# The output product in seven block products with w_out stationary, and sums of h read out of one accumulating bank

## The chip, the cores and the metric

The kernel runs on one core of a Trainium2 chip. The metric is device time in microseconds (us) of one execution. Every execution is put in a state, fast or slow, by its time and the clock that the throttle granted TensorE. PE is TensorE, PEld its weight loads, DVE VectorE, ACT ScalarE, POOL GpSimd. PSUM is the memory that TensorE writes its products into; this kernel uses it as eight banks of 128 x 512 fp32.

## The reference, cut to what matters

A causal convolution of 7 taps (weights by head, softmax over taps), then a two-layer block with Silu, all in fp32:

```python
B, S, D = 8, 4096, 192;  d_ff = 2048          # 32768 tokens
out[b, s] = sum_k softmax(weight)[h, k] * x_pad[b, s + k]      # 7 taps, h = head of the column
h = x @ w_in                                   # (32768,192) @ (192,2048)
g = h * (1.0 / (1.0 + np.exp(-h)))
return (g @ w_out).astype(np.float32)          # (32768,2048) @ (2048,192)
```

## The kernel before

It works in 32 blocks of 1024 tokens. "Up" is the first layer, "down" the second. Up already uses a scheme in which a 2x2 block product takes seven products instead of eight; each product has 64 rows, and two of them run side by side on the halves of the array (in the trace of this kernel both records of a pair start at 1034.82 us, the next pair at 1035.25, 0.43 later). A "slot" is such a pair. VectorE adds the products up from several PSUM banks. Down is plain, with g stationary and w_out moving. In the lines of the profile `ps` is a PSUM bank, `dup` and `win` hold the convolved input and sums of it, `wr` and `ws` come from w_in, `wo` and `wx` from w_out.

```python
gpool = ctx.enter_context(tc.tile_pool(name="gp", bufs=NCH))
upool = ctx.enter_context(tc.tile_pool(name="up", bufs=6))
psum = ctx.enter_context(tc.tile_pool(name="ps", bufs=8, space=PSUM))
# ...
def up_pair(b, j):                       # one of 4 groups of a block: 11 slots
    # P1, P2, E11 in bank "b"; P7, P4, E21 in "c"; P6 in "a"; P5, E22, P3, E12 in "d"
    def after(e, name):
        if name == "P1":
            us[e, 2] = upool.tile([P, TB], F32, tag="u", name="u")
            nc.scalar.copy(us[e, 2], bk[e, "b"])
        elif name == "U2":
            add(us[e, 2], us[e, 2], bk[e, "a"])
        elif name == "U3":
            us[e, 3] = upool.tile([P, TB], F32, tag="u", name="u")
            add(us[e, 3], us[e, 2], bk[e, "c"])
        # ... E22, E21, E12: add(g, us, bank), then Silu in place
# ...
def down(b):
    for i, c in enumerate(order):        # 16 chunks of d_ff
        g = gs.pop((b, c)).rearrange("p n t -> p (n t)")
        for s in range(SUBS):            # 8 times 128 tokens
            nc.tensor.matmul(accs[s // 2][:, s % 2, :], g[:, ts(s, P)], wo[c // 4][:, c % 4, :], ...)
# ...
for b in range(NB):
    # up of b; then turn_in(b+1), load(b+2), conv(b+1), win(b+1); then
    accs = down(b)
    store(b, accs)
```

A tile pool with `bufs=n` hands out n buffers in turn; whoever wants the next one waits until its last reader is done. And the program's text is not the order in which an engine runs: the compiler's scheduler orders each engine's queue itself, within the dependences.

Of the kernel before, what the change touches and what calls it, by code (L numbers as in the profile page):

```python
# [1 line left out]

# [14 lines left out]
def kernel(  # L17
# [22 lines left out]

    nc = tc.nc
# [13 lines left out]
    SUBS = TT // P  # L55
# [8 lines left out]
    out_v = out.rearrange("(n s p) d -> n p s d", s=SUBS, p=P)  # L64

    const = ctx.enter_context(tc.tile_pool(name="const", bufs=1))
    wpool = ctx.enter_context(tc.tile_pool(name="wp", bufs=1))
    xpool = ctx.enter_context(tc.tile_pool(name="xp", bufs=1))
    gpool = ctx.enter_context(tc.tile_pool(name="gp", bufs=NCH))
    upool = ctx.enter_context(tc.tile_pool(name="up", bufs=6))  # L70
    psum = ctx.enter_context(tc.tile_pool(name="ps", bufs=8, space=PSUM))

# [3 lines left out]
    nats, xts, cvs, gs = {}, {}, {}, {}  # L76
# [23 lines left out]
    out32 = moe_w_out.bitcast(I32).rearrange("(q e p) d -> q p e d", e=4, p=P)  # L100
    wr = [const.tile([P, 2, NK, P], F32, name=f"wr{j}") for j in range(NJ)]
    ws = [const.tile([P, 2, NK, P], F32, name=f"ws{j}") for j in range(NJ)]
    wo = [const.tile([P, 4, D], F32, name=f"wo{q}") for q in range(NCH // 4)]
    raws = {}

    def raw_tile(key):
        raws[key] = wpool.tile([P, 2 * WC], I32, tag="raw", name="raw", bufs=2)
        return raws[key]
# [10 lines left out]
    def load_out(q, queue):  # L119
        raw = raw_tile(("o", q))  # L120
        queue.dma_start(out=raw.rearrange("p (e d) -> p e d", e=4), in_=out32[q])

    def rounded(dst, key):
        words = raws.pop(key).rearrange("p (n t) -> p n t", t=2)
        lo, hi = words[:, :, 0], words[:, :, 1]
        ex, st, mh = (
            wpool.tile([P, WC], I32, tag=f"w_{n}", name=f"w_{n}") for n in ("ex", "st", "mh")
        )
# [37 lines left out]
    def round_out(q):  # L166
        rounded(wo[q].rearrange("p e d -> p (e d)"), ("o", q))

    def combine(j):


        def comb(out, u, v, op):
            nc.gpsimd.tensor_tensor(out, u, v, op=op)  # L173

        s, r = ws[j], wr[j]
        comb(s[:, 1, 0, :], s[:, 1, 0, :], s[:, 1, 1, :], ALU.add)
        comb(s[:, 0, 0, :], s[:, 1, 0, :], s[:, 0, 0, :], ALU.subtract)
        comb(s[:, 0, 1, :], s[:, 0, 1, :], s[:, 0, 0, :], ALU.subtract)
        comb(s[:, 0, 2, :], s[:, 0, 2, :], s[:, 1, 2, :], ALU.subtract)
        comb(r[:, 1, 0, :], r[:, 0, 0, :], r[:, 1, 0, :], ALU.subtract)  # L180

# [43 lines left out]
    def turn_in(b):  # L225
        nat = nats.pop(b)
# [5 lines left out]
        for k in range(NK):  # L232
            nc.vector.transpose(  # L233
                xt[:, k, pad : pad + TB], nat[:, k, :, :].rearrange("p k c -> p (k c)")
            )
        nc.sync.dma_start(out=xt[R:P, :, 0:pad], in_=xt[0:R, :, TB : TB + pad])
# [4 lines left out]
    def conv(b, k):  # L241
        if k == 0:
            cvs[b] = xpool.tile([P, NK, TB], F32, tag="cv", name="cv")
            dups[b] = xpool.tile([P, 2, NK, TB], F32, tag="dup", name="dup")
        src, dst = xts[b][:, k, :], cvs[b][:, k, :]
        for i in range(K):
            tap = taps[:, k, i : i + 1]
            if i == 0:
                nc.vector.tensor_scalar(dst, src[:, 0:TB], scalar1=tap, scalar2=None, op0=ALU.mult)
            else:  # L250
                nc.vector.scalar_tensor_tensor(  # L251
                    out=dst, in0=src[:, i : i + TB], scalar=tap, in1=dst, op0=ALU.mult, op1=ALU.add
                )
        for n in range(2):
            for e in range(2):
                nc.sync.dma_start(
                    out=dups[b][R * e : R * e + R, n, k, :], in_=cvs[b][R * n : R * n + R, k, :]
# [19 lines left out]
    def g_tile(b, c):  # L277
        if (b, c) not in gs:
            gs[b, c] = gpool.tile([P, 2, TB], F32, tag="g", name="g")
        return gs[b, c]  # L280

    def up_plain(b, j):
# [7 lines left out]
        for k, (a, n) in order:  # L290
# [8 lines left out]
            if k == NK - 1:  # L299
                for e in range(2):  # L300
                    g = g_tile(b, NM * a + 2 * j + e)
                    nc.scalar.activation(g[:, n, :], hs[a, n, e], AF.Silu)

    def up_pair(b, j):
        d, t = dups[b], wins[b]
        r, s = wr[j], ws[j]

        prods = {
            "P1": (0, r[:, 0, 0, :], d[:, 0, 0, :], "b", True),
            "P2": (0, r[:, 0, 1, :], d[:, 0, 1, :], "b", False),  # L310
            "E11": (0, r[:, 0, 2, :], d[:, 0, 2, :], "b", False),
            "P7": (0, r[:, 1, 0, :], t[:, 2, :], "c", True),
            "P4": (0, r[:, 1, 1, :], t[:, 3, :], "c", False),
            "E21": (0, r[:, 1, 2, :], d[:, 0, 2, :], "c", False),
            "P6": (1, s[:, 0, 0, :], t[:, 1, :], "a", True),
            "P5": (1, s[:, 1, 0, :], t[:, 0, :], "d", True),
            "E22": (1, s[:, 1, 2, :], d[:, 1, 2, :], "d", False),
            "P3": (1, s[:, 0, 1, :], d[:, 1, 1, :], "d", False),
            "E12": (1, s[:, 0, 2, :], d[:, 1, 2, :], "d", False),
        }  # L320
        bk, us = {}, {}

        def mm(e, name):
            other, w, v, bn, first = prods[name]
            half = e ^ other
            if first:
                bk[e, bn] = bank()
            nc.tensor.matmul(  # L328
                bk[e, bn], rows(w, half), rows(v, half), start=first, stop=True,
                skip_group_check=True,  # L330
            )

# [3 lines left out]
        def after(e, name):  # L336
            top, low = 2 * j + e, NM + 2 * j + e
            if name == "P1":
                us[e, 2] = upool.tile([P, TB], F32, tag="u", name="u")
                nc.scalar.copy(us[e, 2], bk[e, "b"])  # L340
            elif name == "E11":
                nc.scalar.activation(g_tile(b, top)[:, 0, :], bk[e, "b"], AF.Silu)  # L342
            elif name == "U2":
                add(us[e, 2], us[e, 2], bk[e, "a"])
            elif name == "U3":
                us[e, 3] = upool.tile([P, TB], F32, tag="u", name="u")
                add(us[e, 3], us[e, 2], bk[e, "c"])
            else:
                c, n, u, bn = {
                    "E22": (low, 1, 3, "d"), "E21": (low, 0, 2, "c"), "E12": (top, 1, 2, "d")  # L350
                }[name]
                g = g_tile(b, c)[:, n, :]
                add(g, us[e, u], bk[e, bn])
                nc.scalar.activation(g, g, AF.Silu)  # L354



        for slot, then in (
            (((0, "P1"), (0, "P6")), ((0, "P1"),)),
            (((0, "P7"), (0, "P5")), ((0, "U2"), (0, "U3"))),  # L360
            (((1, "P6"), (1, "P1")), ((1, "P1"),)),
            (((1, "P5"), (0, "E22")), ((0, "E22"), (1, "U2"))),
            (((1, "E22"), (1, "P7")), ((1, "U3"), (1, "E22"))),
            (((0, "P2"), (1, "P2")), ()),
            (((0, "E11"), (0, "P3")), ((0, "E11"),)),
            (((0, "P4"), (0, "E12")), ((0, "E12"),)),
            (((0, "E21"), (1, "E11")), ((0, "E21"), (1, "E11"))),
            (((1, "P3"), (1, "P4")), ()),
            (((1, "E12"), (1, "E21")), ((1, "E12"), (1, "E21"))),
        ):  # L370
            for e, name in slot:
                mm(e, name)
            for e, name in then:
                after(e, name)

    def down(b):


        accs = [bank()[:, 0 : 2 * D].rearrange("p (s d) -> p s d", s=2) for _ in range(SUBS // 2)]
        order = [NM * a + m for m in range(NM) for a in range(2)]  # L380
        for i, c in enumerate(order):
            g = gs.pop((b, c)).rearrange("p n t -> p (n t)")
            for s in range(SUBS):
                nc.tensor.matmul(  # L384
                    accs[s // 2][:, s % 2, :],
                    g[:, ts(s, P)],
                    wo[c // 4][:, c % 4, :],
                    start=i == 0 and s % 2 == 0,
                    stop=i == NCH - 1,
                    skip_group_check=True,  # L390
                )
        return accs

    def store(b, accs):
        osb = xpool.tile([P, SUBS, D], F32, tag="osb", name="osb")
        for i, acc in enumerate(accs):
            part = osb[:, 2 * i : 2 * i + 2, :]
            if i % 2:
                nc.scalar.copy(part, acc)  # L399
            else:  # L400
                nc.vector.tensor_copy(part, acc)  # L401
        for i in range(2):
            nc.sync.dma_start(out=out_v[b][:, 4 * i : 4 * i + 4, :], in_=osb[:, 4 * i : 4 * i + 4, :])

    turn_in(0)
    load(1)
    conv(0, 0)
    for b in range(NB):
        for j in range(NJ):
            if b == 0:  # L410
                round_in(j)
                if j == 0:
                    for k in range(1, NK):
                        conv(0, k)
# [4 lines left out]
                up_plain(b, j)  # L419
            else:  # L420
                up_pair(b, j)
        if b == 0:
            for q in range(NCH // 4):
                round_out(q)
                if q + 2 < NCH // 4:
                    load_out(q + 2, nc.gpsimd)
# [42 lines left out]
```

## Time and profile before

| | before |
|---|---|
| time, median of 3 runs | 2644.91 us (2644.26 to 2645.23) |
| span of the profiled run, granted clock | 2640.4 us, 0.995 |
| up of one block / down of one block | 38.30 / 41.80 us |
| VectorE busy in a block's up, down (stretches of 38.4 and 41.8 us) | 24.95, 20.29 us |

Read it as: TensorE is the bound in both stages (busy for 38.40 of 38.40 and 41.80 of 41.80 us), and VectorE is idle for 35% of up and about half of down. The lines that say so are in the prediction.

### The profile page before, as it was taken

How to read it: one execution, taken by the hardware profiler on the slowest of the kernel's cores; microseconds unless marked ns; L12 is line 12 of the kernel's file. 1: busy time of each engine (PE TensorE's matmuls, PEld its weight loads, DVE VectorE, ACT ScalarE, POOL GpSimd, SP SyncE). 2: the span in 40 equal slices, each digit the busy share in tenths (PEclk: the TensorE clock that was granted, in tenths of full speed). 3: DMA queues.
4: the chain of work that ended last, by engine and by line, in shares of the span. 5: the costliest groups of instructions: out<-in, count | busy, mean ns of one | idle time of the engine just before them, and what ended most of it. 6: DMA issues, size and time to landing. Idle time of an engine off the chain costs nothing.

```text
span 2640.4 us, 34007 instructions
## 1 busy us (share of the span) xinstructions
PE 2576.4 (98%) x13840; PEld 2045.2 (77%) x13840; DVE 1466.8 (56%) x2270; ACT 780.4 (30%) x1355; POOL 33.7 (1%) x77
## 2 busy tenths in 40 slices
PE   2899999999999999999999999999999999999999
PEld 1777887778887778887778877788877788877788
DVE  7655556555556455556455565555564555564532
ACT  1332223332223332233322233322233322233222
POOL 3000000000000000000000000000000000000000
PEclk9899999999999999999999999999999999999999
DMA  7311211112211212211112211112112122111010
GB/s 150 67 42 31 49 45 33 44 28 46 49 34 39 49 25 49 49 34 40 40 34 48 47 32 43 30 43 49 34 40 49 24 49 49 34 40 34 15 37 13
DMA packets 282220, 111.04 MB, mean 42 GB/s; under 512 B 222160, under 2 KB 255696, under 8 KB 282064
## 3 DMA queue, kind: packets, MB, share of 16 engines
q1 hardware_dynamic: 278912, 100.98, 17.6%
q0 software_dynamic: 1536, 5.51, 0.8%
q10 hardware_dynamic: 1616, 2.39, 0.4%
q8 instruction: 109, 1.79, 0.3%
q14 instruction: 47, 0.39, 0.0%
HBM read 31.49 MB, written 25.17 MB: 21 GB/s over the span
## 4 chain that ended last, share of the span: by engine, by line
PE 97%; DMA 1%; DVE 1%; POOL 0%; ACT 0%; issue 0%; ACTq 0%; SPq 0%; DVEq 0%; POOLq 0%
PE ps L384 51%; PE ps L328 45%; PE ps L292 1%; DVE cv L251 1%; DMA raw<-in_moe_w_in_dram 0%; DMA nat<-in_x_dram 0%; DMA ws<-wr 0%; DMA raw<-in_moe_w_out_dram 0%; POOL ws L173 0%; DMA xt<-xt 0%; DVE w_ex L151 0%; POOL raw L115 0%; DVE w_mh L148 0%; DVE xt L233 0%; DVE w_ex L132 0%
## 5 line engine op out<-in xcount | busy, mean ns | idle before, releaser
L384 PEld LDWEIGHTS ps<-wo,g 128*128 128x128 f32 x8192 | 1330.3, 190 | 24.3 <-issue 24.3
L384 PE MATMUL ps<-wo,g 128*128 128x192 f32 x8192 | 1339.8, 326 | 0.0
L328 PE MATMUL ps<-dup,wr 64*128 64x512 f32 x1984 | 736.9, 591 | 0.0
L328 PE MATMUL ps<-dup,ws 64*128 64x512 f32 x1488 | 679.8, 591 | 0.0
L334 DVE TENSOR_TENSOR g<-u,ps 128x512 f32<-128x512 f32 x744 | 491.4, 684 | 231.6 <-PE ps L328 227.2
L354 ACT ACTIVATE g<-g 128x512 f32<-128x512 f32 x744 | 461.6, 630 | 415.1 <-DVE g L334 414.7
L328 PE MATMUL ps<-win,wr 64*128 64x512 f32 x992 | 505.0, 589 | 0.0
L328 PEld LDWEIGHTS ps<-dup,wr 64*128 64x128 f32 x1984 | 308.9, 187 | 201.0 <-issue 138.0
L334 DVE TENSOR_TENSOR u<-u,ps 128x512 f32<-128x512 f32 x496 | 331.9, 685 | 185.3 <-ACT u L340 170.5
L328 PE MATMUL ps<-win,ws 64*128 64x512 f32 x992 | 427.1, 592 | 0.0
L399 ACT COPY osb<-ps 128x384 f32<-128x384 f32 x64 | 30.6, 478 | 1271.7 <-PE ps L384 1271.7
L251 DVE SCALAR_TENSOR_TENSOR cv<-xt,taps,cv 128x512 f32<-128x512 f32 x576 | 402.2, 750 | 6.4
L328 PEld LDWEIGHTS ps<-dup,ws 64*128 64x128 f32 x1488 | 265.0, 187 | 109.1 <-issue 74.3
L401 DVE COPY osb<-ps 128x384 f32<-128x384 f32 x64 | 35.7, 558 | 517.2 <-PE ps L384 517.2
L328 PEld LDWEIGHTS ps<-win,wr 64*128 64x128 f32 x992 | 185.5, 187 | 90.0 <-issue 50.1
L328 PEld LDWEIGHTS ps<-win,ws 64*128 64x128 f32 x992 | 177.2, 187 | 95.3 <-issue 67.7
L340 ACT COPY u<-ps 128x512 f32<-128x512 f32 x248 | 143.4, 578 | 90.8 <-PE ps L328 90.8
L342 ACT ACTIVATE g<-ps 128x512 f32<-128x512 f32 x248 | 143.5, 579 | 0.0
L272 DVE TENSOR_TENSOR win<-dup 128x512 f32<-128x512 f32 x62 | 42.7, 689 | 126.7 <-DMA dup<-cv 126.7
L292 PE MATMUL ps<-dup,wr 64*128 64x512 f32 x192 | 51.2, 683 | 59.9 <-DMA dup<-cv 46.8
L292 PEld LDWEIGHTS ps<-dup,wr 64*128 64x128 f32 x192 | 39.2, 219 | 71.1 <-DVE w_mh L148 43.4
L272 DVE TENSOR_TENSOR win<-dup,win 128x512 f32<-128x512 f32 x62 | 42.7, 689 | 62.9 <-DMA dup<-cv 62.9
(37 smaller groups left out, 225.7 us busy)
## 6 DMA issues: line engine op xcount, KB each, us to landing
dup<-cv SPq DMA_DIRECT2D x384, 128.0 KB, 2.3
nat<-in_x_dram SPq DMA_DIRECT2D x384, 64.0 KB, 2.5
out_dram<-osb SPq DMA_DIRECT2D x64, 384.0 KB, 2.5
raw<-in_moe_w_out_dram POOLq DMA_DIRECT2D x4, 768.0 KB, 5.7
raw<-in_moe_w_in_dram POOLq DMA_DIRECT2D x12, 192.0 KB, 5.6
ws<-wr ACTq DMA_DIRECT2D x8, 192.0 KB, 4.7
raw<-in_moe_w_in_dram ACTq DMA_DIRECT2D x4, 192.0 KB, 7.8
xt<-xt SPq DMA_DIRECT2D x32, 4.5 KB, 1.9
```

Of the source, the lines that this page charges most:

```text
L251: nc.vector.scalar_tensor_tensor(out=dst, in0=src[:, i : i + TB], scalar=tap, in1=dst, op0=ALU.mult, op1=ALU.add)
L272: nc.vector.tensor_tensor(t[:, i, :], u, v, op=ALU.subtract)
L292: nc.tensor.matmul(hs[a, n, e], rows(wr[j], e)[:, a, k, :], rows(d, e)[:, n, k, :], start=k == 0, stop=k == NK - 1,)
L328: nc.tensor.matmul(bk[e, bn], rows(w, half), rows(v, half), start=first, stop=True, skip_group_check=True,)
L334: nc.vector.tensor_tensor(out, u, v, op=ALU.add)
L340: nc.scalar.copy(us[e, 2], bk[e, "b"])
L342: nc.scalar.activation(g_tile(b, top)[:, 0, :], bk[e, "b"], AF.Silu)
L354: nc.scalar.activation(g, g, AF.Silu)
L384: nc.tensor.matmul(accs[s // 2][:, s % 2, :], g[:, ts(s, P)], wo[c // 4][:, c % 4, :], start=i == 0 and s % 2 == 0, stop=i == NCH - 1, ski ...
L399: nc.scalar.copy(part, acc)
L401: nc.vector.tensor_copy(part, acc)
```

## The change

The intent is to let down use the seven-product scheme too: w_out stationary in 64 columns, so that two products run side by side on the column halves, 44 slots a block. It needs sums of g, which VectorE makes (`sum_g`), and a merge of the partial outputs, which then come out transposed. To free VectorE, up now lets P1, P6, P7, P4 and E21 of a chunk accumulate in one bank, and copies the intermediate sums ("snapshots") out into u tiles, two on ScalarE and one on VectorE. The slots of a whole block are laid out in a string, so that products of one bank lie apart. Store, turn-in and the first part of the convolution are written between the slots of up, a step at every second slot.

```diff
-    upool = ctx.enter_context(tc.tile_pool(name="up", bufs=6))
+    tpool = ctx.enter_context(tc.tile_pool(name="tp", bufs=3))
+    gpool = ctx.enter_context(tc.tile_pool(name="gp", bufs=2 * NJ))
+    upool = ctx.enter_context(tc.tile_pool(name="up", bufs=8))
+    ORDER = (
+        "P1.0 P1.1, P2.3 P1.3, P1.4 P2.0, P6.0 E11.0, "
+        "P1.2 P6.1, P6.4 P6.3, P7.0 P5.0, P6.2 P7.1, "
+        "E11.3 E22.0, E21.0 P7.3, P7.4 E21.1, P7.2 P4.1, "
+        "P4.0 P3.0, E21.4 E12.0, E21.2 E21.3, P4.4 P4.3, "
         # ... 28 more slots
+    def up(b, fill):
         # ... a product P1, P6, P7, P4, E21 of chunk m goes to bank (m, "1")
+        def snap(m, i):
+            us[m, i] = upool.tile([P, TB], F32, tag="u", name="u")
+            if i == 2:
+                nc.vector.tensor_copy(us[m, i], bk[m, "1"])
+            else:
+                nc.scalar.copy(us[m, i], bk[m, "1"])
+        def total(m, a, n, i, bn):
+            g = g_of(m, a, n)
+            nc.vector.tensor_tensor(g, us[m, i], bk[m, bn], op=ALU.add)
+            nc.scalar.activation(g, g, AF.Silu)
+        after = (
+            (("P1",), lambda m: snap(m, 1)),
+            (("P6",), lambda m: snap(m, 2)),
+            (("P7",), lambda m: snap(m, 3)),
+            (("E22", "P7"), lambda m: total(m, 1, 1, 3, "d")),
+            (("P3", "E12"), lambda m: total(m, 0, 1, 2, "d")),
+            (("E11", "P1"), lambda m: total(m, 0, 0, 1, "b")),
+            (("E21", "P4"), lambda m: nc.scalar.activation(g_of(m, 1, 0), bk[m, "1"], AF.Silu)),
+        )
+        for i, slot in enumerate(ORDER.split(", ")):
             # ... the slot's products, what follows them, then
+            fill(i)
+    def sum_g(b, j):                      # four subtractions of 1024 columns into t tiles
+    def down(b, j, accs):
+        def mm(i, half, lhs, rhs, first):
+            nc.tensor.matmul(
+                accs[i][R * half : R * half + R, :], lhs, rhs, ...)     # 64 columns stationary
+    def merge(b, accs):                   # seven copies on ScalarE, six adds on VectorE
+        z, zz = (upool.tile([P, TB], F32, tag="u", name="u") for _ in range(2))
     # ... in the loop over blocks
+            def fill(i):
+                if i >= 36:
+                    if i % 2 == 0:
+                        next(last, None)          # a step of sum_g(b, 0)
+                elif i >= 4 and i % 2 == 0:
+                    next(rest, None)              # a step of store, turn_in, conv(b + 1, 0)
+            up(b, fill)
+        for j in range(NJ):
+            if j:
+                run(sum_g(b, j))
+            down(b, j, accs)
+            # ... conv(b + 1, j + 1), spread, load, win
+        merge(b, accs)
```

## The prediction

> **What bounds the kernel now.** I read the page's busy shares and slices first, then the groups, then the chain of work in order of time, then a timeline of the stage boundary, and last the waits.
>
> The busy shares and slices:
>
> ```profile
> PE 2576.4 (98%) x13840; PEld 2045.2 (77%) x13840; DVE 1466.8 (56%) x2270; ACT 780.4 (30%) x1355; POOL 33.7 (1%) x77
> PE   2899999999999999999999999999999999999999
> PEclk9899999999999999999999999999999999999999
> ```
>
> TensorE is busy in every slice after the start, at full clock. A busy PE does not prove a PE at its peak, so the chain in order of time matters more:
>
> ```profile
> 76.66 34.46 PE ps L292 x144
> 111.12 41.80 PE ps L384 x256
> 152.92 38.30 PE ps L328 x176
> 191.22 41.80 PE ps L384 x256
> ...
> 2594.49 41.81 PE ps L384 x256
> ```
>
> The kernel is 32 blocks of 1024 tokens. The first has a plain first layer; the other 31 have the seven-product first layer (L328, "up") at 38.30 us. All have the second layer (L384, "down") at 41.80 us. Nothing else stands between them: 31 x 38.3 + 32 x 41.8 = 2525 us, plus 111 us until the first down starts, plus 4 us at the end, is the span of 2640 us. So the time is the price of matmuls, and only fewer or better filled matmuls, or a new wait, move it.
>
> ```profile
> L384 PE MATMUL ps<-wo,g 128*128 128x192 f32 x8192 | 1339.8, 326 | 0.0
> L328 PE MATMUL ps<-dup,wr 64*128 64x512 f32 x1984 | 736.9, 591 | 0.0
> L334 DVE TENSOR_TENSOR g<-u,ps 128x512 f32<-128x512 f32 x744 | 491.4, 684 | 231.6 <-PE ps L328 227.2
> L334 DVE TENSOR_TENSOR u<-u,ps 128x512 f32<-128x512 f32 x496 | 331.9, 685 | 185.3 <-ACT u L340 170.5
> L251 DVE SCALAR_TENSOR_TENSOR cv<-xt,taps,cv 128x512 f32<-128x512 f32 x576 | 402.2, 750 | 6.4
> ```
>
> Each fp32 matmul is two records: 8192 for the 4096 of down. A record of 192 columns costs 1339.8 / 8192 = 0.1635 us. In up the timeline shows pairs of 64-row records starting together, then the next pair 0.43 us later:
>
> ```profile
> 1034.82 0.59 PE L328 MATMUL ps<-dup,wr 64*128 64x512 f32 x1
> 1034.82 0.59 PE L328 MATMUL ps<-win,ws 64*128 64x512 f32 x1
> 1035.25 0.59 PE L328 MATMUL ps<-win,wr 64*128 64x512 f32 x1
> 1035.25 0.59 PE L328 MATMUL ps<-win,ws 64*128 64x512 f32 x1
> ```
>
> So two 64-row matmuls run as one. A slot (two fp32 matmuls of 512 columns, side by side) costs 2 x 0.429 = 0.858 us; 44 slots are 37.75 us, against 38.30 measured: up loses only 0.55 us per block to waits and the change of stage. VectorE in one block, from the windows: 20.3 us in down and 25.0 in up.
>
> [...] The kernel before has row tiles only; [...] no run yet shows columns. Its switch between a full array and row tiles twice a block costs at most the 0.55 us above. [...]
>
> **The change part by part.**
>
> *Down.* Removed: 128 matmuls of 192 columns with g stationary, 256 x 0.1633 = 41.8 us. Added: per j 8 + 12 + 2 = 22 matmuls, 128 rows, 64 columns stationary, 512 moving; 88 per block in 44 pairs, neighbours on column halves 0 and 1. If a column pair costs what a row pair costs: 44 x 0.858 = 37.75 us, say 38.1 with a change of mode. Half of the gain is fewer products (44 pairs where a plain scheme with w_out stationary needs 48); the rest is that 48 x 0.858 = 41.2 is already below 41.8. Gain 3.7 us per block. Weight loads have 64 columns instead of 128, and a load of 128 takes 0.187 us, so they stay beside a record of 0.43.
>
> *Up.* Still 88 products in 44 slots. Sums that VectorE made (5 tensor_tensor per chunk, 40 a block) partly move into the bank: P1, P6, P7, P4, E21 accumulate in it and the intermediate sums are copied out. VectorE: one copy and three adds, 32 a block; ScalarE: two copies and four Silu, 48 a block (before 40). Each product after a snapshot now waits for it in the same bank. The order puts 2 to 5 slots (1.7 to 4.3 us) between: P6.0 in slot 3 after P1.0 in slot 0, P7.0 in slot 6, E21.0 in slot 9. A snapshot costs about 0.6 us plus some 0.2 of hand-over, so most are covered.
>
> *VectorE budget.* Back to back, two adds start 0.60 apart, two taps 0.67, transposes 0.63 (1.90 for three). In up: 32 x 0.60 = 19.2; store's three transposes 1.9; turn_in 1.9; seven taps 4.4; sum_g of the first j, four tensor_tensors of 1024 columns [...] 4.6; the last four adds of merge 2.4. Sum 34.4 of 38 us: 90% where it was 65%. In down: three sum_g 13.7, two convs 8.8, win 2.4, merge 1.8: 26.7 of 38. In all 61 of 76 us. ScalarE: 48 x 0.6 + 7 copies x 0.55 = 33 us. Neither exceeds PE, but in up the margin is thin.
>
> *Waits inside down.* sum_g has three t buffers where two sets would be four, so its third operation for j+1 waits for the last uses in j, slot 10 of 11. The first four slots of each j need no sums (3.4 us), and the order of products asks for t[1] only in slot 6, so I let this cost nothing.
>
> *Between the stages.* accs takes five of eight banks. The first three new banks of up are free; the fourth to sixth come from accs 0 to 2, finished 6, 4 and 2.6 us before down ends. The seventh (slot 4, 3.4 us in) is accs 3, read by an add that stands behind one ScalarE copy and two adds after the last product: 0.2 + 0.6 + 3 x 0.65 = 2.75 us. It fits by 0.6 us. For such near misses I charge up 0.8 us: 38.3 + 0.8 = 39.1.
>
> *DMA.* Output goes out in runs of 128 bytes instead of 768 (25 MB, 197 thousand packets, about as many as the input has). The mean share of 16 engines, 15% in the steady stretch, may near 28%. SyncE issues 10 more per block at 0.6 us. All lies beside PE except at the end.
>
> *Start and end.* Before the first down VectorE has another sum_g (4.6 us), but its other work there ends at 96.6 us, 14 us before PE comes: +3 for disorder. The end: merge's last steps 2.8 us, three transposes 1.9, the issue of 8 to 12 stores at 0.6, landing 2.5: about 13 us for 4.
>
> Sum: 114 + 32 x 38.1 (1219) + 31 x 39.1 (1212) + 13 = 2558 us of span; the measured time is 2 to 4 above the span, and I take 6 off because idle VectorE stretches late in down let transposes move forward. **Predicted 2555 us**, 3.4% faster.
>
> **The rivals.**
> (a) *VectorE becomes the bound in up.* For it: 90% of the stage, in-order, with adds that wait for ScalarE. Against: 61 of 76 us over the block, and in the kernel before conv work already ran in down ahead of its use. 2 us more per up would add 62 us: about 2615, within 2%.
> (b) *Column tiles do not run side by side in fp32, or their weight loads do not hide.* For it: no column tile in this trace. Against: [...] loads of 0.19 us that hide behind 0.1635 us records today. Serial tiles would double down (+38 us x 32): near 3750. Exposed loads of 0.1 us per record: 88 x 0.1 = 8.8 us per block: about 2840.
> (c) *The transition stalls.* If up waits for all of merge before its fourth slot, 2 to 3 us per block, 60 to 90 us: 2615 to 2645, the whole gain gone.
> (d) *All hidden.* 44 slots twice at 38.1: 111 + 32 x 38.1 + 31 x 38.3 + 10 = 2528 of span, some 2530.
>
> **Range and chances.** The 2% mark is 2592 us: it takes 38 us more than predicted, 1.2 per block. Rivals (a) and (c) at moderate size lie between 2590 and 2640, (b) far above, (d) below. The order looks laid out for just these waits, so I give 0.73 to faster, 0.19 to the same, 0.08 to slower (nearly all (b)). Range 2518 to 2625.
>
> **What would show it.** Right: in the chain in order of time, down pieces of 37.8 to 38.4 us with 176 records, column-tile records starting in pairs 0.43 apart; up pieces of 38.3 to 40; VectorE above 75% of the span. Wrong: records of down 0.43 apart one by one (b); in the waits, PE or PEld of the products waiting for VectorE (a) or for accs' readers at the start of up (c), by more than 2 us per block in sum.

## The result, and the profile after

Ratios here are the mean time of one kernel's fast runs over that of the other's fast runs of the same rounds, so not quite the ratio of the medians quoted.

| | before | after |
|---|---|---|
| time, median of 4 runs each | 2645.07 us | 3283.93 us (3277.31 to 3288.16) |
| ratio, 95% interval | | 1.2412 (1.239 to 1.2434) |
| granted clock, profiled run | 0.995 | 0.929 |
| a block in the steady stretch | 80.1 us | 101.03 us |

The change made the kernel 24% slower. On the page after, the busy shares and two rows of the slices:

```profile
PE 2882.4 (88%) x11280; PEld 1169.8 (36%) x11280; DVE 2049.5 (62%) x2758; ACT 1013.4 (31%) x1763; POOL 57.4 (2%) x105
PE   3998889888898988989888999889998898988998
PEclk9999998998999999999999999998999999999989
```

TensorE is no longer busy all the time, yet no other engine is full either: VectorE rose from 56% to only 62%. This is not the picture of an engine that has become the bound. It is one of engines that wait for each other. Next the windows over one block, first up, then down. The columns are the stretch, its length, then busy time and instructions of PE, PEld, DVE, ACT and POOL, then the granted clock, the DMA share and GB/s:

```profile
1654.60:1717.70 63.10, 51.77 (x178) 23.38 (x176) 41.02 (x60) 26.93 (x48) 0.20 (x1) 0.89 0.05 9
1616.75:1654.60 37.85, 37.85 (x177) 12.48 (x177) 21.99 (x28) 4.63 (x9) 0.00 (x0) 1.00 0.37 70
```

Down takes what was predicted; all of the loss is in up, which takes 63 us in place of 39. The chain of work in order of time (start, length, what) shows the same, first in block 0 and then in block 16:

```profile
101.06 37.92 PE ps L436 x176
...
1672.76 12.20 PE ps L369 x31
1686.42 7.19 PE ps L369 x27
...
1707.02 10.76 PE ps L369 x34
1717.78 31.93 PE ps L436 x148
```

Where up was one long piece of 176 records before (L328), it (L369) is now in short pieces with other engines' work between them. Down (L436) is 176 records in 37.92 us. The timeline shows the new column tiles in pairs, 0.43 us apart, exactly as the row tiles:

```profile
1649.35 0.59 PE L436 MATMUL ps<-g,wo 128*64 128x512 f32 x1
1649.35 0.59 PE L436 MATMUL ps<-t,wx 128*64 128x512 f32 x1
1649.78 0.59 PE L436 MATMUL ps<-g,wo 128*64 128x512 f32 x1
1649.78 0.59 PE L436 MATMUL ps<-t,wx 128*64 128x512 f32 x1
```

The waits (engine, line, who ended the wait; then total us, times, longest):

```profile
ACT u L379 <- DVE g L386: 451.8, 124, 9.4
PEld ps L369 <- DVE u L377: 281.0, 95, 4.7
PE ps L369 <- DVE u L377: 206.8, 76, 3.9
```

The first line is new and odd. In the kernel before, the like copy waited for its own bank:

```profile
ACT u L340 <- PE ps L328: 90.8, 155, 1.2
```

L379 is ScalarE's snapshot, a copy out of a bank that TensorE has just filled. It reads nothing that VectorE's add (L386) writes. Still that add ends its wait, 124 times, which is 4 in each of 31 blocks, and 3.6 us each on average. What such an add does release is the u tile that it has read: the copy waits for a buffer. (Of the runs below with VectorE's queue repaired, e9 with eight buffers still has this wait, e12 with twelve has none of it.) The other two lines say that matmuls wait for VectorE's snapshot (L377) of their bank. The timeline of one such stretch:

```profile
1662.05 0.69 DVE L377 COPY u<-ps 128x512 f32<-128x512 f32 x1
1662.80 0.69 PE L369 MATMUL ps<-win,wr 64*128 64x512 f32 x1 [2.78 <-DVE u L377]
1666.77 5.34 DVE L283 SCALAR_TENSOR_TENSOR nat<-xt,taps,nat 128x512 f32<-128x512 f32 x7
1672.03 0.68 DVE L386 TENSOR_TENSOR g<-u,ps 128x512 f32<-128x512 f32 x1
1672.74 0.58 ACT L379 COPY u<-ps 128x512 f32<-128x512 f32 x1 [8.74 <-DVE g L386]
1672.76 1.22 PE L369 MATMUL ps<-win,ws 64*128 64x512 f32 x1 [3.01 <-DVE g L386]
```

From 1666.77 on, VectorE does convolution taps of the *next* block (L283) for 5.34 us. Only then comes the add of L386, and in the moment in which it ends, ScalarE's copy (after 8.74 us idle) and a matmul (after 3.01 us) start. VectorE was not short of time, it did work that nobody needed yet while two engines waited. The stretch shows what the order of a queue does here: an add that lets two engines go stood behind 5.34 us of taps.

The matmul after the gap takes 1.22 us where its like take 0.59. That is a second loss: the window from 1672.70 to 1677.00 has a granted clock of

```profile
1672.70:1677.00 4.30, 4.24 (x9) 2.65 (x11) 1.89 (x4) 2.86 (x5) 0.00 (x0) 0.50 0.02 4
```

0.50, a half. The trace has no values of the clock but 0.5 and 1. What brings on the half is not plain from this stretch: after the first gap above (2.78 us) the clock stayed full, and it fell at 1671.67, some 1.9 us into the second (3.01 us), for 6.83 us. Over up the mean clock was 0.89: 0.11 x 63.1 = 6.9 us per block, an estimate, and an upper one, of what the lower clock took, since some of it lay in idle time.

**What the queues hold.** Comparing the instruction order that was emitted for each engine with the text gave two differences. These are read from the emitted queues, not from the profile.

TensorE, after slot 8 ("E11.3 E22.0"):

```
text:     E21.0 P7.3,  P7.4 E21.1,  P7.2 P4.1,  P4.0 P3.0,  E21.4 E12.0, ...
emitted:  P7.3 P7.4,  P2.1 E11.1,  P5.4 E21.0,  P4.0 E21.1,  P7.2 P4.1,  P3.0 E12.0, ...
```

In the emitted order 14 of 87 neighbours are on the same half of the array (in the text 0). In the trace of the change the starts of two such neighbours lie 0.86 us apart, the time of a slot (median of the 254 found at full clock with no wait between them), so most ran one after the other. Counted in slots that is 49 for the text's 44.

VectorE: all 21 taps of the next block stand at the end of down and among the first slots of up. In the text 7 of them are spread over up and 14 lie in down. The sums of g stand ahead of snapshots and adds that they follow in the text.

A count by hand says why TensorE's order was changed. Each snapshot takes a u tile, and its last add gives it back. In the text's order 8 u tiles are alive after slot 5 (counting slots from 0), 9 after slot 6, 11 after slot 7 and 12 after slot 11. The pool has 8, and the merge of the block before holds two of these for a while.

### The profile page after: what moved, and what is told of

It reads as the page before. It is cut to its first block, busy times and chain, and to the rows that moved or that the text cites. A ratio compares the mean times of both kernels' runs of the same rounds, so it can differ in the third digit from the quotient of the medians.

```text
span 3286.4 us, 29826 instructions
## 1 busy us (share of the span) xinstructions
PE 2882.4 (88%) x11280; PEld 1169.8 (36%) x11280; DVE 2049.5 (62%) x2758; ACT 1013.4 (31%) x1763; POOL 57.4 (2%) x105
## 4 chain that ended last, share of the span: by engine, by line
PE 60%; DVE 31%; issue 5%; ACT 3%; DMA 1%; SPq 0%; DVEq 0%; ACTq 0%
PE ps L436 31%; PE ps L369 29%; DVE nat L283 11%; DVE t L427 5%; DVE g L386 4%; DVE u L377 4%; DVE cmb L463 2%; DVE u L463 2%; ACT g L387 1%; DVE nat L281 1%; DVE osb L485 1%; PE ps L331 1%; ACT u L379 1%; DMA nat<-in_x_dram 1%; ACT cmb L465 0%
## 5 line engine op out<-in xcount | busy, mean ns | idle before, releaser
L369 PE MATMUL ps<-dup,ws 64*128 64x512 f32 x2480 | 980.6, 625 | 0.0
L369 PE MATMUL ps<-win,wr 64*128 64x512 f32 x1488 | 761.4, 723 | 230.8 <-DVE u L377 206.8
L436 PE MATMUL ps<-g,wo 128*64 128x512 f32 x3072 | 901.4, 593 | 0.0
L386 DVE TENSOR_TENSOR g<-u,ps 128x512 f32<-128x512 f32 x744 | 495.5, 683 | 640.9 <-PE ps L369 547.9
L369 PE MATMUL ps<-dup,wr 64*128 64x512 f32 x992 | 566.8, 710 | 22.0 <-ACT u L379 20.5
L369 PEld LDWEIGHTS ps<-dup,ws 64*128 64x128 f32 x2480 | 406.3, 202 | 307.7 <-issue 285.4
L427 DVE TENSOR_TENSOR t<-g,t 128x1024 f32<-128x1024 f32 x256 | 313.4, 1224 | 292.0 <-PE ps L436 288.7
L436 PEld LDWEIGHTS ps<-g,wo 128*64 128x64 f32 x3072 | 284.5, 137 | 590.7 <-issue 567.2
L436 PE MATMUL ps<-t,wx 128*64 128x512 f32 x1024 | 481.2, 592 | 0.0
L369 PEld LDWEIGHTS ps<-win,wr 64*128 64x128 f32 x1488 | 284.1, 225 | 539.2 <-DVE u L377 281.0
L379 ACT COPY u<-ps 128x512 f32<-128x512 f32 x496 | 278.6, 583 | 508.2 <-DVE g L386 451.8
L283 DVE SCALAR_TENSOR_TENSOR nat<-xt,taps,nat 128x512 f32<-128x512 f32 x576 | 415.9, 745 | 6.4
L436 PE MATMUL ps<-t,wo 128*64 128x512 f32 x1024 | 372.1, 592 | 0.0
L369 PE MATMUL ps<-win,ws 64*128 64x512 f32 x496 | 292.3, 690 | 89.5 <-DVE g L386 89.5
L427 DVE TENSOR_TENSOR t<-g 128x1024 f32<-128x1024 f32 x256 | 304.9, 1222 | 43.1 <-ACT g L387 43.1
L369 PEld LDWEIGHTS ps<-dup,wr 64*128 64x128 f32 x992 | 188.0, 217 | 203.9 <-issue 93.2
L436 PE MATMUL ps<-g,wx 128*64 128x512 f32 x512 | 240.6, 592 | 0.0
L377 DVE COPY u<-ps 128x512 f32<-128x512 f32 x248 | 166.4, 681 | 0.0
L369 PEld LDWEIGHTS ps<-win,ws 64*128 64x128 f32 x496 | 88.9, 200 | 169.7 <-DVE g L386 115.1
```

The costliest lines, as they stand in the source:

```text
L283: nc.vector.scalar_tensor_tensor(out=dst, in0=src[:, i : i + TB], scalar=tap, in1=dst, op0=ALU.mult, op1=ALU.add)
L369: nc.tensor.matmul(bk[m, bn], rows(w, half), rows(v, half), start=first, stop=True, skip_group_check=True,)
L377: nc.vector.tensor_copy(us[m, i], bk[m, "1"])
L379: nc.scalar.copy(us[m, i], bk[m, "1"])
L386: nc.vector.tensor_tensor(g, us[m, i], bk[m, bn], op=ALU.add)
L427: nc.vector.tensor_tensor(out, u, v, op=ALU.subtract)
```

## The experiments

**Theory A**: the u pool is too small for the laid-out order. **Theory B**: VectorE's queue has work in it that nobody needs yet, ahead of snapshots and adds. Twelve kernels ran in three jobs, each job on one chip with its own runs of the kernel before (medians 2645.03, 2643.73 and 2644.54 us). All results were correct, except for the two kernels that leave out taps.

### e1: twelve u buffers

```diff
-    upool = ctx.enter_context(tc.tile_pool(name="up", bufs=8))
+    upool = ctx.enter_context(tc.tile_pool(name="up", bufs=12))
```

> One edit to the changed kernel: the pool of the copied-out sums (u) has 12 buffers instead of 8. Counting by hand, the laid-out order keeps up to 12 such tiles alive, and with 8 the compiler's scheduler emitted another matmul order in which 14 of 87 neighbours lie on the same row half, so 49 slots of work where the laid-out order has 44; with 12 the emitted TensorE order is the laid-out one. VectorE's order is still the scheduler's, with all 21 conv taps early in the first layer. Theory A (buffers are the cause): up falls from about 63 us to 39 to 42 us, time 2560 to 2650. Theory B (VectorE's order, with conv taps ahead of the adds, is the cause): up stays above 50 us, time above 2900. Theory C (row tiles and column tiles in alternation cost TensorE the time): no change, near 3280.

Measured: 3089.57 us (the median of all four runs), ratio 1.1669 (1.1635 to 1.1702), from fast runs of 3077 to 3095 us with a median of 3084. (A fourth run fell in the slow state, at 3552 us and a clock of 0.744. It was the profiled one, so its trace isn't compared with the others.) TensorE's emitted order was now the text's. So the buffers are a cause, worth 200 us here, but not the greater one: Theory A alone expected at most 2650; the time lies in Theory B's branch, above 2900.

### e2: twelve buffers, and the queues pinned to the text

```diff
+    def keep(ins, key):                  # every PE, DVE and ACT instruction passes here
+        if key in last_of:               # order after its forerunner on the engine; no wait is made
+            tc.add_manual_dep(ins.ins, last_of[key],
+                DependencyInfo(DependencyClass.NoSync, DependencyReason.DATA), reason="order")
+        last_of[key] = ins.ins.name
+        return ins
```

This tells the scheduler to emit an engine's instructions in the order of the text. It makes no wait of its own. The u pool has twelve buffers as in e1. (All instructions then carry this helper's line, L68 or L69.)

> 12 u buffers as in e1_u12, and TensorE, VectorE and ScalarE each kept in the order of the program text by issue-order edges (no waits added). This is what the prediction had assumed of the change. If the prediction failed only because the kernel was not emitted as it reads: 2530 to 2600, centre 2555, up 38.3 to 40 us, down 37.8 to 38.4. If theory B holds, this one gains far more over e1_u12 (over 200 us); if theory A holds alone, the two are within 60 us of each other. If the VectorE budget of 34 us in up was itself too small: above 2650.

Measured: 2560.72 us, ratio 0.9684 (0.9668 to 0.9701), clock 0.988. The chain in the steady stretch is nearly one piece again:

```profile
261.20 73.74 PE ps L68 x340
...
337.52 73.91 PE ps L68 x340
```

The starts lie 76.32 us apart, against 80.1 before and 101.03 after. With the same instructions, in the order in which they were written, the change is 3.2% faster than the kernel before, and over 500 us faster than e1, as Theory B expected (over 200). In block 0 the pin does harm: the first down starts at 141.25 us where it was 101.06.

With 8, 9 or 10 buffers, TensorE pinned to the text does not build (these are builds without a run): the build stops with a deadlock, for ScalarE's snapshot needs a u tile that only a later product can free. With 11 and 12 it builds. That supports the count by hand: the twelfth tile, taken after slot 11, can come late, since the next product of its bank stands in slot 14.

### e3: twelve buffers, pinned, but to the matmul order that eight buffers had

```diff
-        "E11.3 E22.0, E21.0 P7.3, P7.4 E21.1, P7.2 P4.1, "
-        "P4.0 P3.0, E21.4 E12.0, E21.2 E21.3, P4.4 P4.3, "
+        "E11.3 E22.0, P7.3 P7.4, P2.1 E11.1, P5.4 E21.0, "
+        "P4.0 E21.1, P7.2 P4.1, P3.0 E12.0, P2.4 E11.4, "
         # ... and two more lines
```

> As e2_u12_pinned with 12 u buffers and pinned queues, but the 88 products in the order that the changed kernel had emitted with 8 buffers (14 same-half neighbours, 49 slots). This prices the lost pairing without the missing buffers: 5 slots x 0.858 us x 31 blocks = 133 us over e2_u12_pinned if pairing is all there is to the order; over 300 us more if the emitted order itself also makes long waits; none if pairing does not matter.

Measured: 2646.87 us, ratio 1.001 (0.9995 to 1.0025), the same as the kernel before. The order alone costs 2646.87 - 2560.72 = 86 us, or 2.8 per block: the long piece of the chain is 76.52 us where e2 has 73.74. Five lost slots at 0.858 would have been 4.3 per block, 133 in all. The loss is a third below what the count of slots gives; why, no run shows.

### e4 and e7: one tap of seven, with eight and with twelve buffers (results wrong)

```diff
-        for i in range(K):
+        for i in range(1):
```

This takes 18 of 21 taps a block, some 12 us, off VectorE and leaves all else.

> Wrong results on purpose: the changed kernel with 8 u buffers and one conv tap of seven, so VectorE is relieved of 18 operations of 0.67 us (12 us) per block; the matmul order emitted is the same as the changed kernel's. Theory B (VectorE's load and order): falls below 2750. Theory A (buffers and lost pairs): the wait for a u buffer stays but the adds that free it come earlier; 49 slots and the waits keep it above 2850. Both at work: between, 2750 to 2950.

> Wrong results on purpose: e1_u12 (12 u buffers, queues free) with one conv tap of seven, so the 18 tap operations that the scheduler put ahead of adds and copies are gone (12 us per block), while the transposes and the sums of g (t) stay where it put them. If the hoisted taps cause the loss of e1_u12: below 2700. If the hoisted sums of g do: 2800 to 3000. In e4_onetap_u8 the same cut with 8 buffers gave 3154, so the difference to that run is what the buffers alone cost once VectorE has room.

Measured: e4 3154.02 us (ratio 1.1939), in the branch above 2850; e7 2776.14 us (1.0494; 1.0477 to 1.0512), which falls between the branches. In e4 VectorE is busy 53% of the span and the kernel is still 19% slower than before. So what ails it is not VectorE's load. With twelve buffers the taps matter more, 3084 - 2776 = 308 us (median of e1's fast runs), but they are not all of it: e7 is 250 us above e5, below, which has every tap.

### e5 and e6: pin one engine alone, with twelve buffers

```diff
-PINNED = ("PE", "DVE", "ACT")
+PINNED = ("DVE",)        # e6: ("ACT",)
```

> 12 u buffers and VectorE alone kept in the order of the text; TensorE's emitted order is the laid-out one by itself, ScalarE's is the scheduler's and differs a little. Between e1_u12 (3084 us in fast runs) and e2_u12_pinned (2561). If the loss in e1_u12 is VectorE's order: 2540 to 2620. If ScalarE's order carries it: above 2900. TensorE waits less in the start of the kernel than in e2 only if VectorE's pin is not what slowed that.

> The counterpart: 12 u buffers, ScalarE alone kept in the order of the text, VectorE free and in the same emitted order as in e1_u12. If VectorE's order is the cause: 3000 to 3120, as e1_u12. If ScalarE's order is: below 2700.

Measured: e5 2525.47 us, ratio 0.9552 (0.9537 to 0.9566), 15 us below the range for "VectorE's order". e6 3124.52 us, ratio 1.1816 (1.1791 to 1.1841), no better than e1 and 5 us above its range. VectorE's order is the whole of Theory B's loss, ScalarE's none of it.

### e8: as e2, with the pin only from block 1's up on

```diff
     def keep(ins, key):
-        if key in PINNED:
+        if key in PINNED and pinning:
         # ... and ahead of up(b, fill)
+            pinning.append(1)
```

> e2_u12_pinned with the three queues pinned only from the first layer of block 1 on, so that block 0, whose first down started at 141 us in e2 and at 101 in the changed kernel, is left to the scheduler. The steady period of 76.33 us stays: 2560.7 minus 25 to 40: 2520 to 2540.

Measured: **2523.23 us, ratio 0.9542 (0.9528 to 0.9556)**, clock 0.996. It differs from e2 in the start only: the first down is back near 103 us. It is 4.6% faster than the kernel before, with the same arithmetic as the change. It is the lowest time here, but e5, with VectorE alone pinned, is the same within the intervals, and the starts in the steady stretch lie 76.3 us apart in both. Pinning VectorE's queue is enough.

### e9 and e12: no pins, only the early work of VectorE held back, with eight and with twelve buffers

A milder repair, which also tells the causes apart without touching TensorE's queue. Each snapshot, add of `total` and add of `merge` on VectorE is marked; taps, sums of g and transposes get an edge of order (again no wait) behind the one marked last in the text.

```diff
-                nc.vector.tensor_copy(us[m, i], bk[m, "1"])
+                mark(nc.vector.tensor_copy(us[m, i], bk[m, "1"]))
# ... the adds of total and merge likewise
-            nc.vector.tensor_tensor(out, u, v, op=ALU.subtract)
+            held(nc.vector.tensor_tensor(out, u, v, op=ALU.subtract))
# ... the taps of conv and all transposes likewise
```

> The changed kernel with its 8 u buffers, and VectorE's filling work (conv taps, sums of g, transposes) held, by issue-order edges, behind the copy or add that stands before it in the text; the matmul order emitted is the changed kernel's (14 same-half neighbours). It prices the missing buffers once VectorE's order is repaired: the order alone cost 86 us in e3, so 2610 to 2660 if the waits for a u buffer vanish with the hoisted work; 2800 to 3100 if the buffers cost as much by themselves as e4_onetap_u8 (3154) makes it look.

> The same holding with 12 u buffers: the counterpart of e9, and a check that holding the fill alone does what pinning VectorE did in e5 (2525). 2515 to 2545.

Measured: e9 2851.54 us, ratio 1.0783 (1.0767 to 1.0799); e12 2536.33 us, ratio 0.959 (0.9576 to 0.9604). The chain of e12, a whole down and the first piece of the next up:

```profile
178.83 37.92 PE ps L451 x176
216.75 3.68 PE ps L384 x16
```

and its windows, up and down of a later block:

```profile
1216.14:1255.06 38.92, 38.86 (x179) 18.78 (x180) 33.05 (x51) 25.35 (x47) 0.00 (x0) 1.00 0.13 22
1255.06:1292.98 37.92, 37.92 (x178) 12.56 (x178) 28.39 (x35) 5.54 (x10) 1.74 (x1) 1.00 0.33 63
```

Up is 38.92 us, TensorE is busy for 38.86 of these, and VectorE for 33, 85%, without holding it up. e9 has the same VectorE queue rule but eight buffers. The wait for u tiles is there still, 4 times a block, and up is 49 us with a clock of 0.93:

```profile
ACT u L394 <- DVE g L401: 368.1, 124, 7.5
```

```profile
1355.48:1404.72 49.24, 47.66 (x179) 24.07 (x180) 33.75 (x51) 25.70 (x47) 0.00 (x0) 0.93 0.10 17
```

So the buffers cost on their own. Of the 49.24 - 38.92 = 10.3 us that this block loses to e12's, 2.8 are the matmul order (e3) and an estimate of 0.07 x 49.24 = 3.4 is the clock. Of the 4 left, the window shows 49.24 - 47.66 = 1.6 as idle TensorE; where the rest lies is not shown. Clock and waits can't be told apart cleanly, since they come together: the clock is 0.93 in this up and 1.00 in e12's, which has 0.06 us of idle TensorE.

### e10 and e11: twelve buffers, only the taps held, or only the sums of g

> 12 u buffers, only the conv taps held. Of the 560 us between e1_u12 and e5_u12_pin_dve the taps' share: e7_onetap_u12, without taps, kept 250 us of loss, so if it is the sums of g that make the rest: 2700 to 2800. If taps make it all: below 2570.

> 12 u buffers, only the sums of g held. If the two hoistings add up: 3084 minus about 200: 2830 to 2900. If the first stall, by the taps, sets all: above 3000.

e10 leaves the sums and the transposes free, e11 the taps and the transposes of the input and output. Measured: e10 2798.32 us (ratio 1.0582), e11 2809.92 us (1.062). Against 3084 for e1, holding the taps gains 286 us and holding the sums 274, together 560. Holding both and the transposes (e12) gains 548. The two add up, and the transposes are worth nothing that these runs show. e10 is in its expected range, e11 20 us below its own. In e10 the wait that is left at up's matmuls is for VectorE's snapshot, and what was left free to stand ahead of it is the sums:

```profile
PEld ps L384 <- DVE u L392: 202.3, 92, 5.2
```

### The four corners

Times in us (e1 by the median of its fast runs, 3084):

| | VectorE's queue as scheduled | VectorE's early work held |
|---|---|---|
| 8 u buffers | 3284 (the change) | 2852 (e9) |
| 12 u buffers | 3084 (e1) | 2536 (e12) |

The buffers are worth 200 to 315 us and the queue 432 to 548. Either repair alone leaves the kernel slower than before; the two together make it faster by 4.1%, or by 4.5% and 4.6% with pins (e5, e8).

## Why the prediction was wrong

**Down: right.** Predicted 38.1 us a block; 37.92 in the change and in e12. That column tiles of fp32 cost what row tiles do was the estimate; no trace of the kernel before shows one. Here they ran side by side, in pairs of records 0.43 us apart, and rival (b) fell. Their loads, 0.137 us each, were hidden: TensorE was busy for all 37.85 us of the window. A down after row tiles took 37.92 - 37.75 = 0.17 us more than its 44 slots. One reading of the gain was off: fewer products are not half of it but most. By the prediction's own sums, 41.2 - 37.75 = 3.4 us come from 44 slots instead of 48, and 41.8 - 41.2 = 0.6 from the rest.

**Up: wrong by 24 us a block, and this is all of the error.** The step that failed is "The order puts 2 to 5 slots (1.7 to 4.3 us) between", with "so most are covered", and the same step once more in the chances: "The order looks laid out for just these waits". It took the queues to run in the order of the text, so that each snapshot would be prompt. TensorE's and VectorE's did not, and up took 63.10 us instead of 39.1: eight u buffers can't hold the laid-out order, so the scheduler made another for TensorE; and it put taps and sums ahead of snapshots and adds on VectorE. The prediction listed buffers (three t for four, five banks of eight) but never counted those of u, which the change itself raises from 6 to 8, and it could have from the text alone. With both repaired, up takes 38.92 us against the 39.1 predicted, so the sum for up was right; the runs don't split it into its two charges.

**VectorE's budget: right as a sum.** Predicted 34.4 us in up and 26.7 in down, 61 in all; in e12 33.05 and 28.39, or 61.4. Its 4.6 us for four sums of g was the estimate. In the change one took 1.22 us, and back to back they start 1.14 apart (median), 4.56 for four. The budget said nothing on *when* each piece runs. In the change it was done with 41 us in an up of 63, more than planned, since taps had moved there.

**Rival (a), VectorE as the bound, was near the truth and mis-sized.** It charged 2 us per up, for load. The load was no bound: at 53% busy (e4) the kernel was only 4% faster than the change, and at 85% of up (e12) it ran at full speed. What it should have asked is which instruction stands ahead of which in VectorE's queue, whose 2758 instructions ran in the order emitted. The argument against it, that "conv work already ran in down ahead of its use" in the kernel before, was read the wrong way. It was a sign that the scheduler pulls such work ahead: in that kernel's emitted queue 21 taps stand ahead of the adds of a whole up that they follow in the text. Before, that cost nothing that the profile shows; after, more matmuls need VectorE's and ScalarE's copies to be prompt.

**Rival (c), the transition: small.** e12's up is 1.2 us above 44 x 0.858 = 37.75, the charge made (0.55 + 0.8 = 1.35) was of this size. The 0.2 us of hand-over in the prediction's sums was the estimate: in the trace of the change ScalarE starts 0.04 us after the end of the matmul it waited for, and a matmul 0.05 after the end of the copy it waited for (medians of 291 and 66 waits).

**Start and end: a little too dear.** The first down came at 101.06 us, not at 114. The end was as predicted, 13 us: in e12 the last down starts at 2484.43, so it ends 37.92 later at 2522.35, and the span ends at 2535.6. Had the queues run as taken, 2555 would have been about 1% too long: e8 took 2523, e12 2536.

**A cost not thought of: the clock.** The prediction left the clock at full. With gaps of some 3 us in each block, the trace of the change has the clock at a half 83 times, for 3.41 us or a multiple of it (but for the last, which runs past the span's end), 466.5 us in all. After its first block the half clock came during or within 3.4 us after 32 of 44 idle gaps of TensorE of 2.5 to 3.0 us, and all 45 longer ones. Over the span 0.995 - 0.929 = 6.6% more of the cycles were missing than before, about 217 us of 3286 by this estimate. Some of that lay under waits that would have been there anyway, so it can't simply be taken off.

What stays open: why the eight-buffer matmul order costs 86 us rather than 133, how e9's remaining loss splits between waits and clock, and what exactly sets off the half clock (what tells the 32 gaps from the other 12, and why e9's up has 0.93 with 1.6 us of idle TensorE).

## What to carry to other kernels

A laid-out order is worth what its buffers allow: walk through it, count the tiles alive after every step in each pool, and compare with `bufs`; a pool that is too small does not only wait, it makes the scheduler emit another order. Work that is put between the lines to fill gaps must be looked up in the emitted queue of its engine, for an early piece of useful work can delay whoever waits for what stands behind it, at a mean load that looks harmless: here 5.34 us of taps held up two engines with VectorE busy for 62% of the span. When two causes stand behind one loss, test each with the other repaired as well as alone: here each single repair left a kernel slower than before.
